# A planner that holds mixer steps back less, and expects later blocks later

## The chip, the cores and the metric

The kernel runs on one core of a Trainium2 chip. The metric is the device time of one execution in microseconds (us). Times inside the profile count from the first instruction of the profiled execution.

## The reference

Two blocks follow each other. The first is a gated delta rule over 768 steps, for 4 batches of 8 heads with 48 dimensions each; the second is a token and channel mixer over the result, laid out as (4, 768, 384).

```python
k_n = k / (norm(k) + 1e-6)
state = 0                                   # (B, H, 48, 48)
for t in range(768):
    y[t] = q[t] @ state
    state += beta[t] * outer(k_n[t], v[t] - k_n[t] @ state)
x = y as (B, 768, 384)
u = x + (x.T @ U @ V).T                     # rank 32
out = u + relu(u @ w_ch1) @ w_ch2           # 384 -> 1536 -> 384
```

The arithmetic is fp32; some inputs are held in 64-bit floats, and the channel weights are converted on the chip.

## The kernel before, in words

**Work.** The sequence of a batch is cut into 12 chunks of 64 steps. Half a batch, six chunks, is a unit; so there are eight units, n = 0 to 7, two for each batch b. For each unit the kernel loads keys, queries and values (`load_keys`, `load`, `turn_all`), forms the products of keys with keys and queries with keys (`grams`, PSUM tile `p_g`, L561), and inverts a triangular matrix for each chunk and head (`blocks`). The inversion goes: key products to DRAM and back in another layout (`scr`, then `gs`, L633 and L644, issued by SP), norms (L652 to L666, `p_n`), a chain of small subtractions on VectorE (L704 and L710), the result to DRAM and back (L719, then `zt` at L782 or `zt` and `zc` at L731 and L734), and then the halves of a block are joined by matmuls. Units 0 to 2 invert in halves of 16 and join them in three thirds (`join`, tiles `p_e`, `p_d`, `p_x`, `p_v`, L842 to L888). Units 3 to 7 invert blocks of 32 and join once, inside `blocks` (`p_x` L746, `p_v` L760); they return before `("compact", n)` is emitted.

**Recurrence.** `recur(b)` walks the 12 chunks of a batch. A chunk is a chain of three groups of TensorE matmuls with an evacuation after each: `p_y` from the state (L909), VectorE's `rhs` (L936), `p_s` (L943), ScalarE's `z` (L952), `p_s` and `p_y` (L957, L965), VectorE's new state (L980). A unit's first chunk needs its joined blocks, `("below", n, third)`.

**Mixer.** When a batch's recurrence is over, `front(b, i)` makes the rank-32 product and transposes (`p_tt` L1007 and L1016, `p_h` L1031, `p_u` L1041) and `wide(b, i)` the two channel products for half a batch: 36 matmuls into `p_f` (L1080), evacuated by ScalarE's ReLU (L1059), and 36 into `p_o` (L1101), added on VectorE and stored (L1064, L1065). The mixer of a batch runs beside the recurrence of the next.

**What sets the order.** The program is written out by a planner, `run()`. Every part is a generator. It yields `need(...)`, events that it must wait for, or `step(...)`, a piece of work with its estimated cost on each engine (`pe`, `dve`, `act`, `sp`, `pool`), PSUM banks that it takes or gives, and `then`, the time after which its result is expected. `emitted(key, after)` records when an event is expected. The planner keeps a clock for each engine and always emits the step that can start first. `best` is that step; if a part with a lower place, hence more urgent, has a step for the same engine that can start soon enough, that one is emitted instead, and the engine is planned to wait for it:

```python
for other in could:
    early = clock["slow"] > 1.0 or other[1][0] < 5
    if early and engine and other[2] == engine and other[1] < i:
        if other[0] < at + 0.4 * waits[i][engine]:
            best = other
            break
```

`clock["slow"]`, a factor on TensorE's costs, is 1.6 until `front(0, 0)` begins and 1.0 from then on. A mixer step has three products at an estimated 1.95 us; only the `p_f` steps of `wide(0, 1)` are one product each (0.65). Parts with a place of 5 or more (the recurrence of batches 1 to 3, at 5.01 to 5.03, and the blocks of units 3 to 7, at 5.6 and more) are not held for once the mixer runs; unit 2's joins (2.9 to 3.1), the keys, loads and products of units 2 and 3 (below 4), the fronts (1.5) and the evacuations (1) are. The planned clock decides only the order in which instructions stand in each engine's queue; on the chip each engine takes its queue in that order and waits on semaphores.

Of the kernel before, what the change touches and what calls it, by code (L numbers as in the profile page):

```python
# [27 lines left out]
def kernel(  # L28
# [78 lines left out]
    clock = dict(now=0.0, at=0.0, pe=0.0, dve=2.5, act=0.8, sp=0.8, pool=3.8, slow=1.6)  # L107
# [6 lines left out]
    def need(*keys):  # L114

        return [k for k in keys if all(x >= 0 for x in k[1:])]

    def step(pe=0, dve=0, act=0, sp=0, pool=0, then=0.0, on=None, take=(), give=(), ins=64):

        return dict(
            pe=pe, dve=dve, act=act, sp=sp, pool=pool, then=then, on=on, take=take, give=give, ins=ins
        )

    def emitted(key, after=0.0):
        done[key] = clock["at"] + after

    parts, waits, ready = {}, {}, {}

    def advance(i, at):
        clock["at"] = at
        try:
            waits[i], ready[i] = next(parts[i]), at
        except StopIteration:
            del waits[i]
# [9 lines left out]
    def fetched(at, s, goes=False):  # L146

        left = LOT - lot["used"]
        if s["ins"] >= left:
            ahead = s["pe"] * clock["slow"] * left / s["ins"]  # L150
            at = max(at, lot["since"] + FETCH - ahead)
            if goes:
                lot.update(since=at + ahead, used=s["ins"] - left)
        elif goes:
            lot["used"] += s["ins"]
        return at

    def run():

        while waits:  # L160
            best, could = None, []
            for i in sorted(waits):
                while isinstance(waits.get(i), list) and all(k in done for k in waits[i]):
                    advance(i, max([ready[i]] + [done[k] for k in waits[i]]))
                if isinstance(waits.get(i, []), list):
                    continue
                s = waits[i]
                if any(len(free[t]) < s["take"].count(t) for t in s["take"]):
                    continue
                engine = next((e for e in ENGINES if s[e]), None)  # L170
                at = max(
                    [ready[i], clock[engine] if engine else 0.0]
                    + [sorted(free[t])[s["take"].count(t) - 1] for t in s["take"]]
                )
                if s["pe"]:
                    at = fetched(at, s)
                could.append((at, i, engine))
                if best is None or at < best[0] - 1e-6:
                    best = at, i, engine
            if best is None:  # L180
                continue

            at, i, engine = best
            for other in could:
                early = clock["slow"] > 1.0 or other[1][0] < 5
                if early and engine and other[2] == engine and other[1] < i:
                    if other[0] < at + 0.4 * waits[i][engine]:
                        best = other
                        break
            at, i, _ = best  # L190
            s = waits[i]
            for t in s["take"]:
                free[t].remove(min(free[t]))
            ends = {"pe": at}
            if s["pe"]:
                fetched(at, s, True)
                ends["pe"] = clock["pe"] = at + s["pe"] * clock["slow"]
            for e in ENGINES[1:]:
                if s[e]:
                    ends[e] = clock[e] = max(clock[e], ends["pe"]) + s[e]  # L200
            clock["now"] = max(ends.values())
            for t in s["give"]:
                free[t].append(clock["now"] + 0.1)
            advance(i, ends.get(s["on"], clock["now"]) + s["then"])
# [11 lines left out]
    for g in range(2):  # L216
        at = slice(L * g, L * g + L)
# [393 lines left out]
    def blocks(n):  # L611
# [5 lines left out]
        pool, tag = (mix, "ut") if n == 1 else (single, None)  # L617
        def room():

            return [pool.tile([NP, BK + 1, BK], FP32, name=x, tag=tag or x) for x in ("gs", "xt")]  # L620
# [19 lines left out]
        if n > 1:  # L640
            yield need(("inverted", n - 1))
            gs, xt = room()
        yield step(sp=0.4, pool=0.9 if n > 1 else 0, on="sp", then=3.2)
        nc.sync.dma_start(out=gs[:, 0:BK], in_=scr)  # L644
        if n > 1:
            nc.gpsimd.memset(xt, 0.0)
# [133 lines left out]
        yield step(sp=1.1 if n == 0 else 2.2 if n < 2 else 3.2, act=1.1 if n == 0 else 0)  # L780
        for i in range(4):
            two[i % 2].dma_start(out=diagonal(zt, i), in_=blk[i])  # L782
        emitted(("compact", n), 3.2)
        for third in range(3):
            begin(join(n, third, pg, zt), 2.3 + 0.1 * (3 * n + third))

# [21 lines left out]
    def join(n, third, pg, zt):  # L808

        SB, TQ = BK // 2, CS // 3

        bank, ps_of = ("mix", ps_mix) if n < 2 else ("one", ps_one)

        def room(shape, name):
            if n < 2:
                return mix.tile(shape, FP32, name=name, tag="h_f", bufs=12)
            return single.tile(shape, FP32, name=name, tag="xz")

        qs = slice(TQ * third, TQ * third + TQ)
        where = [(e // 4, e // 2 % 2, e % 2) for e in range(TQ * third, TQ * third + TQ)]
        zq = zt.rearrange("p c j r t -> p (c j r) t")[:, qs]

        odd = zq.rearrange("p q (a u s) -> p q a u s", a=2, u=2)[:, :, :, 1]
        yield need(("compact", n))
        if n == 0 and third > 0:
            yield need(("below", 0, 0))
        if (n, third) == (0, 0):
            gated[1] = slice(96, 128), zq[96:128, 0, BK : BK + 1]  # L830
            emitted(("gate", 1))
        if n == 1:
            at = 1536 + TQ * L * third
            zn = early[:, at : at + TQ * L].rearrange("p (q t) -> p q t", q=TQ)
        yield step(pe=0.7 if n < 2 else 0.6, dve=0.0, then=0.1, take=(bank,))
        if n != 1:
            zn = single.tile([128, TQ, L], FP32, name="zn", bufs=2)
        p_e = ps_of([128, TQ, 2, SB], "p_e")
        for e, (c, j, r) in enumerate(where):
            for g in range(2):  # L840
                rows = half(g)
                nc.tensor.matmul(  # L842
                    p_e[rows, e], pg[rows, c, j, r], odd[rows, e], start=True, stop=True
                )

        xe = room([128, TQ, 2, SB], "xe")
        yield step(act=0.65, dve=0.75, then=0.1, give=(bank,))
        turned(zn, zq)
        for a in range(2):
            nc.scalar.mul(xe[:, :, a], p_e[:, :, a], mask_e[:, a : a + 1])  # L850
        yield step(pe=0.7 if n < 2 else 0.6, then=0.1, take=(bank,))
        p_d = ps_of([128, TQ, 2, SB], "p_d")
        for e in range(TQ):
            for g in range(2):
                nc.tensor.matmul(  # L855
                    p_d[half(g), e], zn[half(g), e], xe[half(g), e], start=True, stop=True
                )
        yield step(dve=1.2, then=-0.75, give=(bank,))
        nc.vector.tensor_tensor(out=odd, in0=odd, in1=p_d, op=ALU.subtract)
        turned(zn, zq)  # L860
        yield step(pe=0.7 if n < 2 else 0.6, then=0.1, take=(bank,))
        p_x = ps_of([128, TQ, BK], "p_x")
        for e, (c, j, r) in enumerate(where):
            for g in range(2):
                rows = slice(L * g + BK, L * g + L)
                nc.tensor.matmul(  # L866
                    p_x[L * g : L * g + BK, e],
                    pg[rows, c, j, r, 0:BK],
                    zq[rows, e, BK:L],
                    start=True,  # L870
                    stop=True,
                )
        xz = room([128, TQ, BK], "xz")
        yield step(act=0.75, then=0.1, give=(bank,))
        for g in range(2):
            nc.scalar.copy(xz[L * g : L * g + BK], p_x[L * g : L * g + BK])
        yield step(pe=0.7 if n < 2 else 0.6, then=0.1, take=(bank,))
        p_v = ps_of([128, TQ, BK], "p_v")
        for e in range(TQ):
            for g in range(2):  # L880
                rows = slice(L * g, L * g + BK)
                nc.tensor.matmul(  # L882
                    p_v[rows, e], zn[rows, e, 0:BK], xz[rows, e], start=True, stop=True
                )
        yield step(act=0.75, give=(bank,))
        for g in range(2):
            rows = slice(L * g, L * g + BK)
            nc.scalar.mul(zq[rows, :, BK:L], p_v[rows], -1.0)  # L888
        emitted(("below", n, third), 0.2)
# [232 lines left out]
    for n in range(2, 2 * B):  # L1122
        at = 0.01 * n + (3 if n < 4 else 5)
# [42 lines left out]
```

## Time and profile before

| | |
|---|---|
| median of 6 runs | 666.22 us (663.95 to 668.38) |
| the profiled execution | 665.22 us |
| its span, first to last instruction | 663.5 us |
| mean granted TensorE clock | 0.902 |
| TensorE busy (PE) | 620.1 us, 93% |
| VectorE busy (DVE) | 317.6 us, 48% |
| GpSimd busy (POOL) | 228.6 us, 34% |
| ScalarE busy (ACT) | 169.9 us, 26% |
| DMA | 47.81 MB, mean 72 GB/s |

PE is TensorE's matmuls, PEld its weight loads. The page's second part cuts the span into 40 slices of 16.6 us, and PEclk there is the clock that was granted, in tenths of full speed. The chain is the work that ended last, followed back from the last instruction. In the timeline a row is a group of instructions of one line: start, duration, then in brackets how long the engine sat idle before it and what ended that. A row of stretches gives, for each, its length and then for PE, PEld, DVE, ACT and POOL the busy time with the count of instructions, and at the end the granted clock, the DMA share and GB/s. An fp32 product shows as two matmul records.

### The profile page before, as it was taken

To read this page: it belongs to the slowest core of one execution; us is meant where nothing else is said; L and a number is where in the kernel's file an instruction comes from. 1 tells how busy PE (TensorE), PEld (TensorE's weight loads), DVE (VectorE), ACT (ScalarE), POOL (GpSimd) and SP (SyncE) were. 2 spreads that over 40 slices of the span, in tenths; PEclk is the share of its full clock that TensorE was granted. 3 is DMA by queue.
4 is the path that set the end of the run, shared out by engine and by line. 5 is a ranking of instruction groups with operands and counts; after the bars stand their busy time and mean duration, and the time that the engine had idled before them with its cause. 6 is when DMAs were issued, how large, how long until landed. Compare 5 with 4: busy or idle time off the path is not lost.

```text
span 663.5 us, 19841 instructions
## 1 busy us (share of the span) xinstructions
PE 620.1 (93%) x8736; PEld 399.5 (60%) x8736; DVE 317.6 (48%) x761; ACT 169.9 (26%) x430; POOL 228.6 (34%) x380
## 2 busy tenths in 40 slices
PE   4659997798999999989999999999999999999997
PEld 3548896466765565555556555555565555555554
DVE  3478778786278608845852585348611012000000
ACT  3413454133421331134211321232212211110210
POOL 9544068770671573265519151700000000000000
PEclk9765555598599999999999999999999999999999
DMA  8864358732431371184126223320120000000000
GB/s 119 182 156 84 113 138 198 211 81 72 109 83 41 96 134 29 34 152 81 36 62 129 66 38 72 86 62 2 41 47 14 2 13 12 13 0 25 12 12 25
DMA packets 85159, 47.81 MB, mean 72 GB/s; under 512 B 73584, under 2 KB 78240, under 8 KB 85072
## 3 DMA queue, kind: packets, MB, share of 16 engines
q0 software_dynamic: 14528, 26.98, 17.4%
q1 hardware_dynamic: 65808, 18.86, 13.3%
q8 instruction: 69, 1.13, 0.7%
q10 hardware_dynamic: 4736, 0.69, 0.6%
q14 instruction: 18, 0.15, 0.1%
HBM read 35.49 MB, written 11.01 MB: 70 GB/s over the span
## 4 chain that ended last, share of the span: by engine, by line
PE 86%; DMA 5%; DVE 3%; POOL 3%; issue 2%; ACT 1%; SPq 0%; ACTq 0%; POOLq 0%; DVEq 0%
PE p_f L1080 30%; PE p_o L1101 30%; PE p_y L909 4%; PE p_g L561 3%; PE p_s L943 3%; PE p_s L957 2%; PE p_e L842 2%; PE p_d L855 2%; PE p_y L965 2%; DMA kn<-in_k_dram 1%; PE p_u L1041 1%; PE p_v L882 1%; PE p_h L1031 1%; POOL qn L494 1%; PE p_x L866 1%
## 5 line engine op out<-in xcount | busy, mean ns | idle before, releaser
L1080 PE MATMUL p_f<-ut,w_sb 128*128 128x384 f32 x576 | 204.3, 501 | 0.0
L1101 PE MATMUL p_o<-w_sb,h_f 128*128 128x384 f32 x576 | 203.1, 497 | 0.0
L1080 PEld LDWEIGHTS p_f<-ut,w_sb 128*128 128x128 f32 x576 | 105.4, 191 | 64.7 <-issue 1.2
L1101 PEld LDWEIGHTS p_o<-w_sb,h_f 128*128 128x128 f32 x576 | 104.3, 190 | 65.3 <-issue 2.9
L1059 ACT ACTIVATE h_f<-p_f 128x384 f32<-128x384 f32 x96 | 47.1, 490 | 177.9 <-PE p_f L1080 177.7
L1064 DVE TENSOR_TENSOR x<-x,p_o 128x384 f32<-128x384 f32 x24 | 13.2, 554 | 148.3 <-PE p_o L1101 148.3
L494 POOL DMA_DIRECT2D qn<-in_k_dram x96 | 58.4, 617 | 46.3 <-DVE qt L503 18.3
L710 DVE TENSOR_TENSOR xt<-xt,prod 96x112 f32<-96x112 f32 (+21 forms) x200 | 63.7, 318 | 6.9
L494 POOL DMA_DIRECT2D qn<-in_q_dram x96 | 59.0, 622 | 22.4 <-DVE kt L503 18.5
L433 POOL DMA_DIRECT2D vn<-in_v_dram x64 | 41.9, 666 | 71.8 <-DVE rhs L936 32.7
L704 DVE TENSOR_TENSOR prod<-gs,xt 96x112 f32<-96x112 f32 (+21 forms) x200 | 63.1, 316 | 5.2
L987 ACT COPY x<-p_y 64x192 f32<-64x192 f32 x96 | 30.0, 313 | 55.8 <-PE p_y L965 53.9
L952 ACT COPY z<-p_s 128x192 f32<-128x192 f32 x48 | 15.3, 318 | 94.9 <-PE p_s L943 94.6
L936 DVE TENSOR_TENSOR rhs<-vn,p_y 128x192 f32<-128x192 f32 x44 | 15.4, 350 | 42.8 <-PE p_y L909 42.5
L433 POOL DMA_DIRECT2D kn<-in_k_dram x48 | 31.8, 673 | 2.0 <-DMA qn<-in_q_dram 1.3
L980 DVE TENSOR_TENSOR s<-s,p_s 128x192 f32<-128x192 f32 x40 | 14.0, 351 | 35.7 <-PE p_s L957 29.7
L957 PEld LDWEIGHTS p_s<-z,kn 64*64 64x64 f32 x704 | 17.4, 153 | 22.6 <-issue 16.3
L943 PEld LDWEIGHTS p_s<-rhs,zt 64*64 64x64 f32 x704 | 16.9, 153 | 23.2 <-issue 16.1
L909 PEld LDWEIGHTS p_y<-s,kt 48*64 48x64 f32 x704 | 17.5, 153 | 20.6 <-issue 8.7
L957 PE MATMUL p_s<-z,kn 64*64 64x48 f32 x704 | 23.0, 248 | 4.5 <-ACT z L952 4.5
L943 PE MATMUL p_s<-rhs,zt 64*64 64x48 f32 x704 | 22.6, 248 | 4.5 <-DVE rhs L936 4.5
L909 PE MATMUL p_y<-s,kt 48*64 48x48 f32 x704 | 23.4, 248 | 2.3 <-ACT x L987 1.8
(126 smaller groups left out, 638.4 us busy)
## 6 DMA issues: line engine op xcount, KB each, us to landing
wide<-in_moe_w_ch_dram POOLq DMA_DIRECT2D x7, 768.0 KB, 5.5
vn<-in_v_dram POOLq DMA_DIRECT2D x64, 72.0 KB, 3.2
out_dram<-x SPq DMA_DIRECT2D x24, 192.0 KB
kn<-in_k_dram POOLq DMA_DIRECT2D x48, 72.0 KB, 3.6
gs<-scr SPq DMA_DIRECT2D x8, 384.0 KB
scr<-xt SPq DMA_DIRECT2D x8, 384.0 KB
scr<-pg SPq DMA_DIRECT2D x30, 96.0 KB
zt<-scr SPq DMA_DIRECT2D x30, 96.0 KB
```

The source lines that it names most:

```text
L433: engines[queue].dma_start(out=t[half(g ^ (s % 2) if crossed else g), :, s], in_=src[b, 4 * g + s, hf * UC * L : (hf + 1) * UC * L, :].rea ...
L494: nc.gpsimd.dma_start(out=places[rows, x, j, :, 0 : ds.stop - ds.start], in_=src[b, h, hf * UC * L : (hf + 1) * UC * L, ds].rearrange("(m ...
L561: nc.tensor.matmul(p_g[par][to, c, j], kq[0][rows, x, j, c0 + c], kq[i][rows, x, j, c0 + c], start=True, stop=True,)
L704: nc.vector.tensor_tensor(out=prod, in0=gb[:, :, j : j + 1, j + 1 :].to_broadcast([NP, split, m, w]), in1=xb[:, :, 0:m, j : j + 1].to_broa ...
L710: nc.vector.tensor_tensor(out=xb[:, :, 0:m, j + 1 :], in0=xb[:, :, 0:m, j + 1 :], in1=prod, op=ALU.subtract,)
L909: nc.tensor.matmul(p[half(x ^ par), par, D * (2 * i + j) : D * (2 * i + j) + D], kq[i][half(par, D), x, j, cu], s_old[half(par, D), x, j], ...
L943: nc.tensor.matmul(p_s[half(x), par, D * (2 + j) : D * (2 + j) + D], zt[half(x ^ par), cu, j, par], rhs[half(x ^ par), 2 * j + par], start ...
L957: nc.tensor.matmul(p_s[half(par), x, D * j : D * j + D], kn[half(x), cu, 2 * j + par], z[half(x), 2 * j + par], start=True, stop=True,)
L987: nc.scalar.copy(tokens_of(b, c, g), pair_of(p_y, 1)[half(g)])
L1059: nc.scalar.activation(hs[f], p_f, ACTF.Relu)
L1080: nc.tensor.matmul(p_f, w1_sb[:, t, f * 128 : (f + 1) * 128], ut[:, t], start=(t == 0), stop=(t == KT - 1),)
L1101: nc.tensor.matmul(p_os[c], hs[e][:, c * 128 : c * 128 + 128], w2_sb[:, e], start=(e == 0), stop=(e == FT - 1),)
```

## The change

It has four parts. The planner's wait for a more urgent step stays 0.4 of the waiting step's cost until the mixer runs, and is at most 0.1 us from then on. For units 2 to 7 the load of `gs` is expected after 4.9 us instead of 3.2. For unit 2 `("compact", n)` is expected after 4.7 us instead of 3.2. And in the joins of unit 2 the result of each matmul group is expected after 0.4 us instead of 0.1, in all four groups. No instruction is added or removed, and no tile or queue is changed: only the order in each queue.

```diff
@@ run()
             for other in could:
                 early = clock["slow"] > 1.0 or other[1][0] < 5
                 if early and engine and other[2] == engine and other[1] < i:
-                    if other[0] < at + 0.4 * waits[i][engine]:
+                    wait = 0.4 * waits[i][engine]
+                    if other[0] < at + (wait if clock["slow"] > 1.0 else min(wait, 0.1)):
                         best = other
                         break
@@ blocks(n)
-        yield step(sp=0.4, pool=0.9 if n > 1 else 0, on="sp", then=3.2)
+        yield step(sp=0.4, pool=0.9 if n > 1 else 0, on="sp", then=3.2 if n < 2 else 4.9)
         nc.sync.dma_start(out=gs[:, 0:BK], in_=scr)
...
-        emitted(("compact", n), 3.2)
+        emitted(("compact", n), 3.2 if n < 2 else 4.7)
@@ join(n, third, pg, zt): the steps of p_e, p_d, p_x and p_v
-        yield step(pe=0.7 if n < 2 else 0.6, dve=0.0, then=0.1, take=(bank,))
+        yield step(pe=0.7 if n < 2 else 0.6, dve=0.0, then=0.4 if n > 1 else 0.1, take=(bank,))
...
-        yield step(pe=0.7 if n < 2 else 0.6, then=0.1, take=(bank,))
+        yield step(pe=0.7 if n < 2 else 0.6, then=0.4 if n > 1 else 0.1, take=(bank,))
```

The line numbers in the text are those of the kernel before; from the second line of the edit in `run()` on, a line of the changed kernel stands one further down.

More of the change, by code (lines that the diff above doesn't have):

```diff
@@ L860, in join @@
         turned(zn, zq)
-        yield step(pe=0.7 if n < 2 else 0.6, then=0.1, take=(bank,))
+        yield step(pe=0.7 if n < 2 else 0.6, then=0.4 if n > 1 else 0.1, take=(bank,))
         p_x = ps_of([128, TQ, BK], "p_x")
@@ L876, in join @@
             nc.scalar.copy(xz[L * g : L * g + BK], p_x[L * g : L * g + BK])
-        yield step(pe=0.7 if n < 2 else 0.6, then=0.1, take=(bank,))
+        yield step(pe=0.7 if n < 2 else 0.6, then=0.4 if n > 1 else 0.1, take=(bank,))
         p_v = ps_of([128, TQ, BK], "p_v")
```

## The prediction

> **What bounds the kernel now.** I read the page first: busy shares, slices, chain.
>
> ```profile
> PE 620.1 (93%) x8736; PEld 399.5 (60%) x8736; DVE 317.6 (48%) x761; ACT 169.9 (26%) x430; POOL 228.6 (34%) x380
> PE   4659997798999999989999999999999999999997
> PEclk9765555598599999999999999999999999999999
> PE 86%; DMA 5%; DVE 3%; POOL 3%; issue 2%; ACT 1%; SPq 0%; ACTq 0%; POOLq 0%; DVEq 0%
> ```
>
> TensorE holds 86% of the chain, and from slice 12 (counted from 0; 200 us) it is all but full. Its work is the same before and after (576 p_f and p_o products, 288 each), so a new order can gain or lose in three ways only: time in which PE idles, time at the half clock (the 5 in PEclk), and breaks in the mixer's stream. The change acts once the mixer runs (128 us on), so the second 5 of PEclk, slice 10, is the first place to look. The timeline of PE there (start, us, engine, line, operation, count of records; an fp32 product is two):
>
> ```profile
> 156.09 2.06 PE L842 MATMUL p_e<-zt,pg 64*64 64x32 f32 x64
> 157.98 1.10 PE L855 MATMUL p_d<-xe,zn 64*64 64x32 f32 x32
> 159.87 1.92 PE L855 MATMUL p_d<-xe,zn 64*64 64x32 f32 x32 [0.78 <-ACT xe L850]
> 161.71 1.92 PE L866 MATMUL p_x<-zt,pg 32*32 32x32 f32 x64
> ...
> 165.62 1.06 PE L882 MATMUL p_v<-xz,zn 32*32 32x32 f32 x32 [0.89 <-ACT xz L876]
> ...
> 175.87 4.21 PE L1080 MATMUL p_f<-ut,w_sb 128*128 128x384 f32 x6
> 180.00 0.58 PE L943 MATMUL p_s<-vn,zt 64*64 64x48 f32 x16
> 180.52 2.20 PE L1080 MATMUL p_f<-ut,w_sb 128*128 128x384 f32 x6
> ```
>
> Unit 2's joins run as one block from 156.05, with no mixer product between them. The second p_d takes 1.92 for what took 1.10 before, and three p_f products take 4.13 (175.94 to 180.07) where 2.13 is normal: the block runs at half clock. Windows of one clock step (3.41 us) show where it falls and where it does not:
>
> ```profile
> 156.53:159.94 3.41, 2.63 (x90) 2.51 (x88) 0.78 (x2) 1.41 (x5) 0.00 (x0) 0.99 0.03 5
> 159.94:163.36 3.42, 3.42 (x94) 3.36 (x96) 1.85 (x4) 0.47 (x2) 0.00 (x0) 0.50 0.00 0
> 286.22:289.63 3.41, 2.33 (x71) 1.46 (x64) 2.13 (x2) 1.00 (x4) 2.30 (x4) 1.00 0.57 158
> ```
>
> The first (PE busy 2.63, all small tiles) costs the clock; it comes back at 180.42. The third is busy for less (2.33) and keeps it; some 1.1 of that is wide p_tt. So the mix counts, not only busy time. That third window is the end of the recurrence of batch 1, where the mixer of batch 0 has run out:
>
> ```profile
> 283.94 0.45 PE L943 MATMUL p_s<-rhs,zt 64*64 64x48 f32 x16
> 284.88 0.45 PE L957 MATMUL p_s<-z,kn 64*64 64x48 f32 x16 [0.49 <-ACT z L952]
> 285.93 0.45 PE L909 MATMUL p_y<-s,kt 48*64 48x48 f32 x16 [0.37 <-DVE s L980]
> 287.18 0.45 PE L943 MATMUL p_s<-rhs,zt 64*64 64x48 f32 x16 [0.57 <-DVE rhs L936]
> 288.14 0.45 PE L965 MATMUL p_y<-z,qk 64*64 64x48 f32 x16 [0.51 <-ACT z L952]
> 288.52 1.66 PE L1007 MATMUL p_tt<-x,u_sb 128*32 128x384 f32 x12
> ```
>
> Each uncovered link of the recurrence leaves PE idle for 0.4 to 0.6.
>
> **What the Trainium skill says.** "TensorE: Matmul & The Clock Gate", section "What's actually happening", has the clock halved after an idle window of about 3.4 us and restored after a busy one, the windows free-running. The trace agrees: the half-clock stretch from 159.94 to 180.42 is 20.48, six windows. It also shows that a window of small matmuls (2.63 of 3.41) counts as idle. The same page, table of specifications, has ScalarE and VectorE as strict FIFO; here ACT and DVE wait only for the head of their order, as the idle entries show. So I follow each queue below.
>
> **The change, part by part.** The orders of the two built programs differ only from the first front on.
>
> 1. *Holding back.* A mixer step (three products, model cost 1.95) was held for a more urgent one due within 0.4 x 1.95 = 0.78; now within 0.1. The old order of unit 2's joins was p_e 32, p_d 32, p_x 32, p_v 32, p_e 16, key products (p_g) 16, p_d 16, p_x 16, p_g 16, p_v 16, p_g 16, then p_f. The new one puts three p_f after the first p_e, after p_d with p_g, after p_x with p_g and a half of p_v, and then three p_o between nearly all the rest. p_e starts after the same 27 p_f products (about 156), after the landing that ended a wait at 154.66, so the later due times alone move nothing there.
>    Price: elapsed 156.05 to 180.07 is 24.0, for 112 join products, 48 p_g and 3 p_f. At full clock, without the waits: p_e 2.0 + 1.0 and p_d 1.93 + 0.96 (rows at 156.09 and 157.98); p_x and p_v 1.9 together, from unit 4's p_x, the same 32*32 tiles, 96 records from 296.93 to 297.87 at full clock (p_v likewise); p_g 48 at 0.59 per 16 = 1.77 (row at 290.11); p_f 2.13. Sum 11.7. **Gain 12.3** if the clock holds; not below 2, since the three waits (0.78, 0.89, 0.52) get 2 us of mixer as cover. I take 12.3: the worst new window, p_d 32 with p_g 32, has 1.2 of dense 64-wide p_g and at least 0.2 of p_f in it, more than the window that kept the clock has beside its p_tt.
>    Behind the moved steps, with the new order laid out from 156 by these durations: on DVE the keys' transpose of unit 3 (1.77) now precedes the two transposes of joins; p_d has 2.1 of p_f as cover. The third join's subtraction waits for p_d to about 174 with the last weight slice's five passes (4.0) queued behind it; they end near 179, p_o of f = 9 to 11 comes near 187, and norm (L654), behind them, near 182, p_n near 184. ACT's norm (L652) for unit 3 stands ahead of a join's copy: key products end near 167, the gs load takes 10 from there as before (176.6 to 186.4), so it is there at 177 to 178, when ACT reaches it. All held, by 1 to 6 us.
> 2. *Breaks.* The mixer's stream is cut into 131 runs instead of 125. Three products after a small group take 2.13, in a run 23.22 / 12 = 1.94: 6 x 0.19 = **loss 1.1**.
> 3. *Front of batch 0.* Two query groups stand ahead of p_h, and p_f between the transposes covers the 0.29 wait at 140.13: **gain 0.3**, between -1 (p_h waits for the qk products on DVE) and 0.5.
> 4. *End of the recurrence of batch 1.* The mixer of batch 0 is used up earlier: the new order has two more links uncovered, so idle 0.49 + 0.37 + 0.1 more than the 1.94 shown. Then unit 4's blocks: DVE transposes zc at 298.49, released by the DMA, and p_v (L760) runs at 301.50. Inversion end to that transpose is 285.47 to 298.49, 13.0, none of it PE's. All of unit 4's chain moves up with its PE inputs by about 10, but p_x and p_v now stand directly behind p_u and p_h without p_f between: wait about 2.5. And now 6 to 7 us pass with recurrence tiles and p_g alone and 2.9 idle, so a free-running window can fall wholly inside and cost the clock. From p_tt to p_u it then takes 124.01 to 136.13 = 12.1 as in the first front at half clock, against 288.52 to 295.78 = 7.3: 4.8 more, part of which covers the wait of 2.5. **Loss 1 to 8; I take 5.**
> 5. *Later due times (gs 4.9, compact 4.7, joins 0.4) and queues.* No order of units 3 to 7 has the joins any more (L724 returns before). gs moves p_n one recurrence step later, beside mixer products. On SP the beta load of unit 3 (3.06 of issue) goes behind gs: SP sits idle from 153 to 176 anyway, and beta lands 3.6 after, near 181, for use near 182. On POOL the xt memsets (1.0) shift by two to eight query loads of 0.62; POOL is idle for 15 at a time there. Zero, with 1 us either way: their cover is the 9 or so us between the DMA's end and p_x in units 5 to 7.
> 6. *Fronts of batches 2 and 3.* p_o between the transposes covers waits of 0.24 at 433.97, 554.22 and 560.58: **gain 0.5** (0 to 0.7). From 567 on both orders are the same 96 us of mixer.
>
> Sum: 12.3 - 1.1 + 0.3 - 5.0 + 0.5 = 7.0. The profiled execution took 665.22 (span 663.5 and 1.7 around it), so 658.2; the median of the runs, 666.22, is 1.0 above it: **659.2**.
>
> **Rivals.**
> - *The clock holds at item 4 too*: loss 1 to 2 there, total gain 10 to 11, about 656. For it: 286.22 kept its clock. Chance 0.27, against 0.40 for the forecast.
> - *The clock falls in the joins anyway.* Then one to three groups of p_f and p_o run at 4.13 rather than 2.13, item 1 brings about 4, and the sum is 4 - 1.1 + 0.3 - 5 + 0.5, a loss of 1.3: 667.5. For it: 40 to 128 us stay at half clock with PE 97% busy at 80 to 100. Against: after p_f at 175.94 it recovered at once. Chance 0.17.
> - *Slower: unit 4's chain does not move up.* If its gs or zc transfers stay put (their SP queue is nearly packed, 226.87 to 246.2), p_v cannot come before 299, while 6 fewer mixer products are done by then; the 12 of item 1 are lost in that wait, and breaks and half clock remain: 4 more, 670. It decides once the chain moves up by less than 5. Against: inversion 3 begins after p_n, which moves with PE. Chance 0.11.
> - Anything else 0.05; that the order does not change is excluded by the built programs.
>
> **The numbers.** A measurement of this kernel can tell about 0.5%, 3.3 us: faster means below 662.9, slower above 669.5. Faster: 0.37 of the 0.40, all of 0.27, 0.03 of the third and a part of the rest, 0.68. Slower 0.12, same 0.20. The range leaves out the slow rival and little else: 654.5 to 667.5; the forecast's own is 657 to 662.5.
>
> **What would show it.** Right: no 5 in PEclk after slice 7; no p_f or p_o group of 4 us between 156 and 185; the first p_tt of batch 1 near 278; idle before p_v of unit 4. Wrong at step 1: half clock between 160 and 180 again. Wrong at step 4: no idle and no half clock between 270 and 295 (faster than forecast), or p_tt near 278 but the first p_s of batch 2 still near 306.

## The result, and the profile after

| | before | after |
|---|---|---|
| median of all runs beside each other | 665.16 us (661.52 to 674.59, 72 runs) | 661.65 us (655.07 to 666.69, 35 runs) |
| ratio after/before, 95% interval | | 0.9926 [0.9909, 0.9943] |
| profiled execution / its span | 665.22 / 663.5 us | 666.69 / 664.9 us |
| mean granted TensorE clock | 0.902 | 0.897 |

The change makes the kernel faster by 0.74%, some 4.9 us (0.0074 x 665.16). The ratios, and the medians of the clock further down, leave out the runs that were more than 1.5% above the fastest of their kernel, four of the 35 here; the medians in the table keep them and differ by 3.5 us. The profiled execution of the changed kernel is the longest of its 35 runs, so its trace shows where time can be lost and not what a usual run loses. The page of the changed kernel, the same lines as before:

```profile
PE 621.1 (93%) x8736; PEld 398.5 (60%) x8736; DVE 317.8 (48%) x761; ACT 169.8 (26%) x430; POOL 228.5 (34%) x380
PE   4659897699999999889999999999999999999997
PEclk9755555679999999958999999999999999999999
PE 86%; DMA 7%; DVE 4%; ACT 1%; SPq 1%; issue 1%; POOL 0%; ACTq 0%; DVEq 0%
```

The 5 of slice 10 has gone from PEclk. In its place there is a low clock in slices 17 and 18 (283 to 316 us), where before had 9s. In this profile the clock in unit 2's joins was won for all but one window, and a new loss came at the end of batch 1's recurrence. The timeline of PE in the changed kernel, first the joins (start, us, engine, line, operation, records):

```profile
156.68 2.06 PE L843 MATMUL p_e<-zt,pg 64*64 64x32 f32 x64
158.67 2.20 PE L1081 MATMUL p_f<-ut,w_sb 128*128 128x384 f32 x6
160.80 1.12 PE L856 MATMUL p_d<-xe,zn 64*64 64x32 f32 x32
162.71 1.06 PE L856 MATMUL p_d<-xe,zn 64*64 64x32 f32 x29 [0.79 <-ACT xe L851]
...
165.32 3.20 PE L1081 MATMUL p_f<-ut,w_sb 128*128 128x384 f32 x6
168.45 1.20 PE L867 MATMUL p_x<-zt,pg 32*32 32x32 f32 x64
...
184.06 4.14 PE L1102 MATMUL p_o<-w_sb,h_f 128*128 128x384 f32 x12
```

Mixer products now stand between the join groups. One p_f group takes 3.20 where 2.20 is normal: the clock was at half from 164.0 to 167.4, one window, against six (159.9 to 180.4) before. Then the end of the recurrence of batch 1:

```profile
275.27 0.45 PE L958 MATMUL p_s<-z,kn 64*64 64x48 f32 x16
275.54 0.41 PE L966 MATMUL p_y<-z,qk 64*64 64x48 f32 x16
276.27 0.45 PE L910 MATMUL p_y<-s,kt 48*64 48x48 f32 x16 [0.31 <-DVE s L981]
...
276.77 0.66 PE L562 MATMUL p_g<-qt,kt 48*64 48x64 f32 x32
279.01 0.45 PE L944 MATMUL p_s<-rhs,zt 64*64 64x48 f32 x16 [1.59 <-DVE prod L705]
279.94 0.68 PE L958 MATMUL p_s<-z,kn 64*64 64x48 f32 x16 [0.48 <-ACT z L953]
...
284.67 2.77 PE L1008 MATMUL p_tt<-x,u_sb 128*32 128x384 f32 x12
...
302.33 2.88 PE L1081 MATMUL p_f<-ut,w_sb 128*128 128x384 f32 x6
```

More links stand without a mixer product than before, and the wait of 1.59 is new: a product `p_g` of unit 4's queries stands ahead of `p_s`. VectorE finishes evacuating it (`qk`, 278.12 to 278.86) just before `p_s` starts, with small steps of unit 4's inversion ahead of that. From 279.94 on the small groups take 0.68 where they took 0.45; the clock comes back at 303.9. The stretches show it: first the window of one clock step that ended at 280.05, then what followed (length, PE busy and count, PEld, DVE, ACT, POOL, granted clock, DMA share, GB/s):

```profile
276.64:280.05 3.41, 1.34 (x75) 1.11 (x69) 3.17 (x13) 0.34 (x2) 0.00 (x0) 0.99 0.18 62
160.59:164.00 3.41, 2.62 (x89) 2.31 (x91) 1.26 (x3) 1.00 (x3) 2.62 (x5) 0.99 0.37 64
280.00:304.00 24.00, 21.55 (x425) 13.93 (x426) 7.31 (x14) 7.50 (x18) 20.60 (x33) 0.50 0.77 148
```

PE was busy for 1.34 of 3.41 us ahead of the long loss, and for 2.62 ahead of the one-window loss in the joins. During the long one it was busy for 21.55 of 24 us and still stayed at half clock.

Cut at the same marks of TensorE's order, the two profiles differ so (us):

| stretch | before | after |
|---|---|---|
| start to p_tt of batch 0 | 124.0 | 123.8 |
| to p_e of unit 2 | 32.1 | 32.9 |
| to p_tt of batch 1 | 132.4 | 128.0 |
| to p_tt of batch 2 | 130.4 (132 mixer products) | 133.4 (126) |
| to p_tt of batch 3 | 125.2 | 124.5 |
| to the end | 119.4 (168) | 122.3 (174) |

### The profile page after: what moved, and what is told of

It reads as the page before. It is cut to its first block, busy times and chain, and to the rows that moved or that the text cites. A ratio compares the mean times of both kernels' runs of the same rounds, so it can differ in the third digit from the quotient of the medians.

```text
span 664.9 us, 19849 instructions
## 1 busy us (share of the span) xinstructions
PE 621.1 (93%) x8736; PEld 398.5 (60%) x8736; DVE 317.8 (48%) x761; ACT 169.8 (26%) x430; POOL 228.5 (34%) x380
## 3 DMA queue, kind: packets, MB, share of 16 engines
q8 instruction: 69, 1.13, 0.7%
## 4 chain that ended last, share of the span: by engine, by line
PE 86%; DMA 7%; DVE 4%; ACT 1%; SPq 1%; issue 1%; POOL 0%; ACTq 0%; DVEq 0%
PE p_f L1081 30%; PE p_o L1102 30%; PE p_y L910 4%; PE p_g L562 3%; PE p_s L944 3%; PE p_s L958 2%; PE p_e L843 2%; PE p_y L966 2%; PE p_u L1042 2%; PE p_d L856 1%; DMA scr<-pg 1%; DMA zt<-scr 1%; DMA gs<-scr 1%; PE p_h L1032 1%; DMA kn<-in_k_dram 1%; DMA scr<-xt 1%
## 5 line engine op out<-in xcount | busy, mean ns | idle before, releaser
L1081 PE MATMUL p_f<-ut,w_sb 128*128 128x384 f32 x576 | 207.3, 505 | 0.0
L495 POOL DMA_DIRECT2D qn<-in_q_dram x96 | 58.9, 621 | 10.2 <-DVE kt L504 7.1
L958 PEld LDWEIGHTS p_s<-z,kn 64*64 64x64 f32 x704 | 17.7, 155 | 19.6 <-issue 15.2
```

The costliest lines, as they stand in the source:

```text
L495: nc.gpsimd.dma_start(out=places[rows, x, j, :, 0 : ds.stop - ds.start], in_=src[b, h, hf * UC * L : (hf + 1) * UC * L, ds].rearrange("(m ...
L958: nc.tensor.matmul(p_s[half(par), x, D * j : D * j + D], kn[half(x), cu, 2 * j + par], z[half(x), 2 * j + par], start=True, stop=True,)
L1081: nc.tensor.matmul(p_f, w1_sb[:, t, f * 128 : (f + 1) * 128], ut[:, t], start=(t == 0), stop=(t == KT - 1),)
```

## The experiments

Two theories were tested. **The first**, that of the prediction: the shorter holding back puts mixer products between the join groups, which is the gain, and it uses up the mixer before batch 1's recurrence ends, which is the loss; the due times do nothing. **The rival**: the due times bring the gain. Each experiment ran on the same chip as the kernel before. A mixer product in an unbroken run of them is 0.645 us (two records of 128x384 at 0.3225).

**hold**: only the holding back.

```diff
-                    if other[0] < at + 0.4 * waits[i][engine]:
+                    wait = 0.4 * waits[i][engine]
+                    if other[0] < at + (wait if clock["slow"] > 1.0 else min(wait, 0.1)):
```

> Only the planner's wait is capped at 0.1; the due times are those of before. Theory (the gain is the clock in unit 2's joins, part of it lost again at the end of batch 1's recurrence): its joins have the mixer between them as in the changed kernel, and its last five links of that recurrence are uncovered too, so it takes what the changed kernel takes, 658 to 663. Rival (the later due times bring the gain): no gain, 664 to 666.

Measured: 664.07 us, ratio 0.9955 [0.9928, 0.9981]. The median lies above the 658 to 663 of the theory and within the 664 to 666 of the rival. The interval still leaves out 1, so there is a gain, but a smaller one than forecast. The order is as expected. In the profile p_f groups stand between the joins, one of them partly at half clock, and the last links are bare:

```profile
160.00 2.20 PE L1081 MATMUL p_f<-ut,w_sb 128*128 128x384 f32 x6
166.54 3.32 PE L1081 MATMUL p_f<-ut,w_sb 128*128 128x384 f32 x6
...
280.82 0.45 PE L944 MATMUL p_s<-rhs,zt 64*64 64x48 f32 x16 [1.15 <-DVE qk L578]
286.50 2.77 PE L1008 MATMUL p_tt<-x,u_sb 128*32 128x384 f32 x12
```

The clock was at half from 281.5 to 291.7, so the loss at the end of the recurrence is there in this profile too.

**due**: only the three due times.

```diff
-        yield step(sp=0.4, pool=0.9 if n > 1 else 0, on="sp", then=3.2)
+        yield step(sp=0.4, pool=0.9 if n > 1 else 0, on="sp", then=3.2 if n < 2 else 4.9)
...
-        emitted(("compact", n), 3.2)
+        emitted(("compact", n), 3.2 if n < 2 else 4.7)
...
-        yield step(pe=0.7 if n < 2 else 0.6, then=0.1, take=(bank,))
+        yield step(pe=0.7 if n < 2 else 0.6, then=0.4 if n > 1 else 0.1, take=(bank,))
```

> Only the later due times; the planner's wait is 0.4 of a step as before. Its joins of unit 2 stand nearly in one block again (p_e 32, p_g, p_d 32, p_g, p_x 32, p_v 32), but every link at the end of batch 1's recurrence has three mixer products beside it. Theory: half clock in the joins as before, no gain there; 3 to 5 gained at the end of batch 1's recurrence; 660 to 663. Rival (due times do nothing by themselves): 664 to 666. Rival (they bring the whole gain): as the changed kernel or faster, with the clock held between 160 and 180.

Measured: 659.59 us, ratio 0.9901 [0.9863, 0.9939]. The due times alone bring as much as the whole change (the intervals overlap), and the holding back alone brings less. The clock fell in its joins for one window (163.8 to 167.2) and not for six as before. The timeline of PE in this kernel, at the end of batch 1's recurrence:

```profile
270.07 2.20 PE L1101 MATMUL p_o<-w_sb,h_f 128*128 128x384 f32 x6
272.20 0.45 PE L943 MATMUL p_s<-rhs,zt 64*64 64x48 f32 x16
272.58 2.20 PE L1101 MATMUL p_o<-w_sb,h_f 128*128 128x384 f32 x6
274.71 0.45 PE L965 MATMUL p_y<-z,qk 64*64 64x48 f32 x16
275.09 2.20 PE L1101 MATMUL p_o<-w_sb,h_f 128*128 128x384 f32 x6
277.22 1.48 PE L1007 MATMUL p_tt<-x,u_sb 128*32 128x384 f32 x12
```

Every one of the last links has a mixer group beside it, and no idle entry stands in brackets. In the order of this kernel the recurrence of batch 1 begins after 27 products of batch 0's mixer, in the changed kernel after 36: nine more are left to cover its end.

**filljoin**: the kernel before with an unused matmul of 128x384 after each group in unit 2's three joins, 12 in all (7.7 us at 0.645), to see what the lost clock there costs.

```diff
+    def fill(cols=384):
+        p_fill = ps_mix([128, cols], "p_fill")
+        nc.tensor.matmul(p_fill, ident, w1_sb[:, 0, 0:cols], start=True, stop=True)
...
+        if n == 2:
+            fill()
```

> The kernel before, with one wide matmul (128x384, its result is not used) after each of the 12 groups of unit 2's joins; the order is otherwise the same. It adds 12 x 0.65 = 7.7 of work and hides at most the 2.2 of waits there. Theory (the clock counts): full clock through the joins gives back some 8 to 10, so 663 to 667 and no half clock between 160 and 180. Rival (what the mixer products bring in the changed kernel is cover for waits): 670 to 672.

Measured: 668.85 us, ratio 1.0042 [1.002, 1.0065], between the two forecasts. The clock stayed at full from 128.1 to the end in its profile. An added matmul takes more there than 0.645, though: from its start to the next one's it is 0.84, between two small groups.

```profile
155.17 0.91 PE L810 MATMUL p_fill<-w_sb,ident 128*128 128x384 f32 x2
156.01 1.12 PE L846 MATMUL p_e<-zt,pg 64*64 64x32 f32 x32
```

The 12 take 10.2 together and cost 2.8 (0.0042 x 665.65), so about 7 came back. Up to 2.2 of that are waits of the joins that the added work filled (0.78, 0.89 and 0.52 in the profile before). The clock lost in before's joins is thus worth an estimated 5 to 7 us of a usual run, less than the 10 that half of its 20.5 us would be.

**fillend**: the changed kernel with six unused matmuls of 128x256 at the uncovered links of batch 1's recurrence (`fill()` as above, with 256 columns). They were reckoned at 0.43 us each; in its profile each takes 0.63 from its start to the next one's, 3.8 in all.

```diff
+                if b == 1 and c > 9:
+                    fill()
...
+            if b == 1 and c > 9:
+                fill()
...
+            if b == 1 and c in (9, 10):
+                fill()
```

> The changed kernel, with six matmuls of 128x256 (0.43 each, result not used) beside the uncovered links at the end of batch 1's recurrence; all else in the same order. Theory (the loss there is half clock, 24 us of it in the profile of the changed kernel): the clock holds, 4 to 7 faster than the changed kernel, 655 to 658. Rival (the loss is waits and unit 4's chain of blocks, which do not depend on the clock): the same as the changed kernel or up to 2 slower, 661 to 664.

Measured: 657.02 us, ratio 0.9862 [0.9835, 0.9889]. With more work the kernel is faster than the changed kernel by 0.64% (0.9926 less 0.9862), 4.3 us. The timeline of PE shows why; p_fill is the added matmul:

```profile
273.98 0.70 PE L908 MATMUL p_fill<-w_sb,ident 128*128 128x256 f32 x2
274.61 0.69 PE L562 MATMUL p_g<-qt,kt 48*64 48x64 f32 x32
276.27 0.45 PE L950 MATMUL p_s<-rhs,zt 64*64 64x48 f32 x16 [0.97 <-DVE prod L705]
...
281.15 1.66 PE L1018 MATMUL p_tt<-x,u_sb 128*32 128x384 f32 x12
...
292.70 2.10 PE L1091 MATMUL p_f<-ut,w_sb 128*128 128x384 f32 x6
```

The clock is full here throughout: p_tt takes 1.66 (2.77 in the changed kernel) and the first p_f 2.10 (2.88). From p_tt to that p_f it is 11.6 us instead of 17.7. The 0.97 in front of p_s is left.

**fillend_qlate**: the same, with unit 4's third query product held until the recurrence is over, so that it can't stand in front of p_s.

```diff
+            if n == 4 and c0 == 4:
+                yield need(("rec", 3))
```

> The changed kernel with the six extra matmuls at the end of batch 1's recurrence, and with unit 4's third query product moved behind that recurrence. In the changed kernel it stood between p_y and p_s, took the PSUM pair that p_s needs, and p_s waited 1.59 for its evacuation. Theory: 1 to 2 faster than with the extra matmuls alone, 655 to 656. Rival (unit 4's chain of blocks sets the start of batch 2's recurrence anyway): no difference, 657.

Measured: 658.15 us, ratio 0.9895 [0.9856, 0.9933], not separable from fillend. In its profile p_s starts at 275.74 with no idle entry, so that product was the cause of the wait. But the planner also moved other steps (129 products instead of 126 between the p_tt of batches 1 and 2), so what the 0.97 costs in time stays open.

**gs_only**: only the due time of units 2 to 7's `gs`.

```diff
-        yield step(sp=0.4, pool=0.9 if n > 1 else 0, on="sp", then=3.2)
+        yield step(sp=0.4, pool=0.9 if n > 1 else 0, on="sp", then=3.2 if n < 2 else 4.9)
```

> Only the later gs time (4.9). Unit 2's joins stand in one block as before, 23 mixer products stand between unit 4's key products and unit 3's p_x, and the last five links of batch 1's recurrence have no mixer product beside them. Theory: no gain, and 0 to 4 lost at the end of that recurrence, 665 to 669. Rival (it is this part that the due times' gain comes from): 658 to 662.

Measured: 667.64 us, ratio 1.0037 [1.0018, 1.0057], slower. Its order leaves the joins' block as it was and more of batch 1's last links bare (seven idle entries there, 3.25 us, where before had four with 1.94); its profile, which is one of its longest runs, has the half clock in both places, 20.5 and 23.9 us.

**cj_only**: only the two due times of unit 2, the compact blocks' (4.7) and the join groups' (0.4).

```diff
-        emitted(("compact", n), 3.2)
+        emitted(("compact", n), 3.2 if n < 2 else 4.7)
...
-        yield step(pe=0.7 if n < 2 else 0.6, then=0.1, take=(bank,))
+        yield step(pe=0.7 if n < 2 else 0.6, then=0.4 if n > 1 else 0.1, take=(bank,))
```

> Only the two due times of unit 2 (compact 4.7, joins 0.4); gs and the planner's wait as before. Theory (what the due times bring is the cover at the end of batch 1's recurrence, and it comes from unit 2's joins, since batch 1's recurrence starts with fewer mixer products used up): as with all due times, 658 to 662. Rival (the gs time of the later units brings it): no gain, 664 to 667.

Measured: 656.84 us, ratio 0.9881 [0.9836, 0.9926]: at least as much as the whole change, the intervals overlapping.

**compact_only** and **join_only**: one of those two each.

> Only the due time of unit 2's compact blocks (3.2 to 4.7) is changed. Both due times of unit 2 together gave 0.9881 [0.9836, 0.9926]. Theory A (the gain of the pair is a covered end of batch 1's recurrence and mixer products put beside the joins, and the compact blocks' due time alone is enough for both, since its order has one product at each of the last links and the key products stand between the join groups): 0.988 to 0.992, the profile's stretch from p_e of unit 2 to batch 1's p_tt near 124 us, the clock lost for one window at most in the joins and none near 280. Theory B (the joins' own due times carry it): 0.997 to 1.003. Theory C (only the two together give it): both this and the joins' due time alone within 0.995 to 1.0.

> Only the due time of what a join's groups release (0.1 to 0.4, unit 2) is changed. In its order products of the mixer and key products stand between the join groups, but the last links of batch 1's recurrence stand uncovered, as in the changed kernel. Theory A (the compact blocks' due time carries the gain, by the cover at the end of the recurrence): 0.995 to 1.003, with the clock lost from about 280 us for some windows. Theory B (the joins' own due times carry it, the uncovered links costing little on average): 0.986 to 0.991.

Measured: compact_only 663.18 us, 0.996 [0.9938, 0.9983]; join_only 660.11 us, 0.9906 [0.987, 0.9942]. The theory that the compact blocks' due time carries the gain by its covered end fell. The joins' own due time carries most, though the two intervals just touch. The timelines of PE tell the two apart; first compact_only:

```profile
162.51 1.87 PE L842 MATMUL p_e<-zt,pg 64*64 64x32 f32 x32
164.31 1.06 PE L882 MATMUL p_v<-xz,zn 32*32 32x32 f32 x32
166.44 1.80 PE L855 MATMUL p_d<-xe,zn 64*64 64x32 f32 x29 [1.06 <-ACT xe L850]
...
169.97 4.21 PE L1080 MATMUL p_f<-ut,w_sb 128*128 128x384 f32 x6
```

No mixer product stands between these groups, and the p_f that follows takes 4.21: half clock from 161.1 to 174.8, four windows. Then join_only:

```profile
154.27 2.20 PE L1080 MATMUL p_f<-ut,w_sb 128*128 128x384 f32 x6
156.41 1.12 PE L855 MATMUL p_d<-xe,zn 64*64 64x32 f32 x32
158.31 1.06 PE L855 MATMUL p_d<-xe,zn 64*64 64x32 f32 x29 [0.79 <-ACT xe L850]
...
160.32 2.20 PE L1080 MATMUL p_f<-ut,w_sb 128*128 128x384 f32 x6
162.46 1.20 PE L866 MATMUL p_x<-zt,pg 32*32 32x32 f32 x64
163.59 0.69 PE L561 MATMUL p_g<-kt 48*64 48x64 f32 x32
164.21 0.69 PE L882 MATMUL p_v<-xz,zn 32*32 32x32 f32 x32
164.84 2.20 PE L1080 MATMUL p_f<-ut,w_sb 128*128 128x384 f32 x6
```

A p_f group stands after every one to three kinds of small matmuls, and none takes more than 2.20. With the same products in each stretch as before, p_e of unit 2 to p_tt of batch 1 takes 125.0 us (152.29 to 277.34) instead of 132.4. Its last links are uncovered, and they cost one window of clock in its profile (276.3 to 279.7).

**hold_cj**: the changed kernel with the gathers' due time set back, so the holding back and unit 2's two due times together.

```diff
-        yield step(sp=0.4, pool=0.9 if n > 1 else 0, on="sp", then=3.2 if n < 2 else 4.9)
+        yield step(sp=0.4, pool=0.9 if n > 1 else 0, on="sp", then=3.2)
```

> The changed kernel with the due time of unit 3's gathers set back to 3.2 (left are the cap on the holding back and both due times of unit 2). Its TensorE order is nearly that of the changed kernel, with the end of batch 1's recurrence uncovered. Theory A (the cap spends the mixer's products early and so takes part of the gain of the two due times): 0.991 to 0.995, as the changed kernel's 0.9926. Theory B (it was the gathers' due time, slower alone at 1.0037, that took it): 0.986 to 0.990, as the two due times alone.

Measured: 661.28 us, ratio 0.9921 [0.9889, 0.9953], the changed kernel's own figure. This points to the holding back, and not the gathers' due time, as what takes from the gain: 0.9881 without it, 0.9921 with it. It is not shown, since the two intervals overlap.

**due_fill** and **cj_fill**: the three due times, and unit 2's two, each with three unused matmuls of 128x256 where a join group waits for ScalarE.

```diff
+        if n == 2 and third == 0:
+            fill()
...
+        if n == 2 and third == 1:
+            fill()
...
+        if n == 2 and third == 0:
+            fill()
```

> The kernel with the later due times alone, with three matmuls of 128x256 (0.43 each, result not used) at the three waits of PE in unit 2's joins (0.79, 0.38, 0.89 in its profile). Theory (the clock falls in the joins in most runs and costs 2 to 4): 656 to 659, 1 to 3 faster than without them. Rival (the joins no longer matter): 659 to 661.

> The two due times of unit 2 alone, and three more matmuls of 128x256 (0.43 us each, results not used) in unit 2's join groups that wait for ScalarE (1.3 us of work added). Theory A (these waits trip the clock once, for 3.4 us, which costs some 1.7 us, and the added work lies mostly in idle time): 0.984 to 0.988, 653 to 657 us; no half-clock stretch after the first one. Theory B (nothing is left to lose in the joins once key products stand between their groups): 0.988 to 0.991, the added work being paid in full.

Measured: due_fill 655.81 us, 0.9857 [0.9818, 0.9895]; cj_fill 657.62 us, 0.9878 [0.9848, 0.9909]. In cj_fill's profile the clock stayed at full from 129.6 on. Neither differs from its version without the added matmuls (0.9901 and 0.9881) by more than the intervals, 2 to 3 us wide on each side, so what the one window costs that due's and cj_only's profiles lose stays open. The lowest ratios are those of due_fill, fillend, cj_fill and cj_only, 0.9857 to 0.9881, not separable from each other. The intervals of the first two lie below the changed kernel's; those of the other two reach into it, or up to it. cj_only needs no added work.

**What the profiles have in common.** Half-clock time, in us, in the profiles of the kernels that have the same TensorE work (what falls into the last 2 us is left out):

| kernel | first stretches, up to 142 at most | near unit 2's joins | end of batch 1's recurrence | sum | span | ratio of the runs |
|---|---|---|---|---|---|---|
| before | 109.2 | 20.5 | 0 | 129.7 | 663.5 | 1 |
| after | 102.4 | 6.8 (front) + 3.4 | 23.9 | 136.5 | 664.9 | 0.9926 |
| hold | 122.9 | 3.4 | 10.2 | 136.5 | 662.0 | 0.9955 |
| due | 99.0 | 3.4 | 0 | 102.4 | 653.1 | 0.9901 |
| gs_only | 119.5 | 20.5 | 23.9 | 163.8 | 674.9 | 1.0037 |
| cj_only | 102.4 | 3.4 | 0 | 105.8 | 653.8 | 0.9881 |
| compact_only | 102.4 | 13.7 | 0 | 116.1 | 657.9 | 0.996 |
| join_only | 102.4 | 0 | 3.4 | 105.8 | 653.3 | 0.9906 |
| hold_cj | 102.4 | 6.8 (front) + 3.4 | 10.2 | 122.9 | 661.7 | 0.9921 |

A straight line through before's point with 0.37 us of span for each us at half clock gives the other spans within 1.4 us, hold alone being off by 4.0 (gs_only: 34.1 x 0.37 = 12.6, measured 11.4; due: -27.3 x 0.37 = -10.1, measured -10.4). The Trainium skill, "TensorE: Matmul & The Clock Gate", section "Terms", prices time at half clock at one half of itself; 0.37 is below that, which fits a TensorE that also waits in these stretches. The first column is lost almost wholly in work that stands in the same order in all of these kernels, and still it differs by 24 us (99.0 to 122.9). That is as large as the effects sought, so one profile of each kernel can rank the mechanisms but not size them; the ratios do that.

**What the other runs show.** The mean granted clock of every run is on record, and 2 x (1 - clock) x span is the run's half-clock time (changed kernel, profiled: 2 x 0.1027 x 664.9 = 136.6, against 136.5 in the table). Medians over the runs, less the medians of the kernel before beside them, in us:

| kernel | half-clock time | span |
|---|---|---|
| hold | -5.5 | -1.9 |
| due | -13.7 | -6.1 |
| gs_only | +8.9 | +2.0 |
| cj_only | -18.3 | -9.4 |
| compact_only | -6.7 | -2.8 |
| join_only | -14.2 | -5.8 |
| hold_cj | -10.2 | -5.9 |
| filljoin (work added) | -18.9 | +3.1 |
| fillend (work added) | -28.2 | -9.4 |

A few runs whose record reads 0.98 or more without their being faster are left out. 0.45 us of span for each us at half clock gives the seven without added work within 2.1. So the link of time and clock is not one of single profiles only. Within the runs of one kernel the slope is 0.24 (286 runs taken together), so part of what parts the kernels is something else that goes with the clock, waits that the same order covers for one; how much is not settled. The median of the changed kernel is 114.1 us and that of fillend 98.5. A usual run of the changed kernel thus loses some 16 us of clock that the six matmuls keep, and not the 34.1 of its profile (6.8, 3.4 and 23.9).

**Do the parts add?** The three due times do: -0.94% (joins), -0.40% (compact blocks) and +0.37% (gathers) sum to -0.97%, measured together -0.99%, each of these known to 0.2 to 0.4%. The holding back doesn't: -0.45% and -0.99% would give -1.44%, measured -0.74%. In both orders of the joins, hold's and join_only's, p_f groups stand after p_e and after p_d with p_g, so the second part finds little left to gain there. That explains why the gains don't add, and not why hold brings less than join_only: the last links of both are bare. Their orders also differ in the fronts, where hold has query products ahead of p_h, and in one more bare link; which of these takes from hold's gain was not tried.

## Why the prediction was right or wrong

**The total was right**, 659.2 with 654.5 to 667.5, against 661.65, and faster as forecast: 4.9 us by the ratio against 7.0 of the sum. The reason for it was half right, and that the total came out near is in part luck: the joins were priced too high by 4 us or more, and the due times, worth 6.6 us by themselves (0.0099 x 665.65), at nothing. Of the four signs that were to show it right one came, no p_f group of 4 us between 156 and 185. A 5 stands in slice 17, the first p_tt of batch 1 came at 284.67 and not near 278, and no idle entry stands before p_v of unit 4.

- **Item 1, joins, +12.3: mis-sized.** In the changed kernel 156.68 to 184.12 is 27.4; less five of its six groups of three mixer products at 2.13 (10.7; the sixth has its like in before's stretch), and less 1.0 for recurrence groups, the same joins took 15.7, against 24.0: 8.3 gained in these two profiles. Three terms failed. p_x and p_v were priced by unit 4's 96-record groups; the row at 168.45 has 64 in 1.13 (to the next start at 169.58), and with four rows of 32 at 0.62 the 192 records took 3.6 and not 1.9. One window lost the clock (1.7), and one wait of 0.79 stayed. In usual runs it may be less again: in filljoin only about 7 came back in all. (The 112 join products of the text should be 192, as its own list adds up; the sum does not use the figure.)
- **Item 5, later due times, zero: wrong, and the main error.** The sentence that the later due times "alone move nothing there" was argued from when p_e starts. They do not move p_e; they move what stands between the groups after it, since a group that is expected 0.3 later lets a mixer step go first. join_only is -0.94% on its own. I had compared only the two whole orders and gave the difference to the edit that reads most like it. Nor did the orders differ only from the first front on: with the later gathers ScalarE takes the recurrence's z ahead of unit 2's norm at 116.54, where before had norm first.
- **Item 4, end of batch 1's recurrence, -5: right in kind, and in size for the usual run.** The clock did fall there, in the profile for 23.9 us. That profile lost about 9.9: 6.9 from p_tt to p_tt (133.4, plus 3.9 for six products fewer, less 130.4) and 3.0 in the links ahead. fillend puts the usual loss at 4.3 or more. The wait of unit 4's chain (2.5) did not come; its p_x stands at 297.18 with no wait entry. The chain moved up by 5.2 and not by 10, and with the clock at half the first p_s of batch 2 came only 1.0 earlier (305.80 instead of 306.80). The new wait was another: 1.59 for VectorE behind p_g, which no step had.
- **Item 3, +0.3: wrong sign in this profile.** From p_tt to p_e it took 32.9 instead of 32.1; a p_f group at 136.18 took 4.11, at half clock from 133.3 to 140.1. But that stretch took 30 to 36 us in the other runs, so the size is not settled. **Item 6, +0.5:** 0.7 from p_tt of batch 2 to that of batch 3 (125.2 to 124.5). **Item 2, -1.1:** not tried by itself.
- **The rivals.** That the clock holds at the end of the recurrence happened in no profile of a kernel with the holding back, unless work was added there (fillend). That it falls in the joins anyway happened for one window. Unit 4's chain did move up, by little more than the 5 that this rival named: its last small subtraction ended at 280.29 instead of 285.47.

What stays open: where a usual run of the changed kernel loses its clock, since the other runs have only the mean; what the holding back costs besides; and what the 1.59 wait costs by itself.

## What to carry to other kernels

When a planner's constants are changed together, build each constant alone before giving the gain to one: here the edits overlapped, and unit 2's two due times without the other two edits were at least as good as all four. Where small matmuls stand in a block, ask what wide matmul follows each of them, and whether work that is put there is missing as cover later. Size a clock effect by the ratio of many runs, since much the same work lost between 99 and 123 us of clock before the change acts.

## What the runs showed of the hardware

- **Busy time alone does not decide whether a window keeps the clock.** Of stretches of one window, those of before (2.63 busy, shown with the prediction) and the changed kernel (2.62, shown above) lost it; in join_only a window that lies in the joins too kept it (the rows are cut within 0.22 us of the clock's own steps):

```profile
272.63:276.04 3.41, 1.99 (x96) 1.65 (x96) 1.66 (x6) 0.95 (x3) 0.12 (x1) 1.00 0.41 119
...
156.69:160.10 3.41, 2.62 (x120) 2.51 (x120) 1.72 (x4) 1.92 (x5) 2.85 (x5) 1.00 0.30 62
```

  The second row has the same 2.62 and kept the clock. The first row, the uncovered links, lost it from 276.3 on. One measure parts the windows better: the rows of the array that each matmul record uses times the columns that it streams (128 x 384 for p_f, 64 x 32 for p_e), summed over a window. Cut at the clock's own steps, from 125 to 560 us in the fourteen profiles, the 16 windows that lost the clock have 98 to 233 thousand (before 178, the changed kernel's joins 211), and of the 1690 that kept it all but four (205 to 212) have more than 233 (join_only 291). These sums are estimates from the durations of the traces, and no run varies the measure by itself. The Trainium skill, "TensorE: Matmul & The Clock Gate", section "What's actually happening", speaks of an idle window; here windows with PE busy for three quarters counted as such.
- **A lost clock can stay lost under load.** PE was busy for 21.55 of 24.0 us in the changed kernel and the clock came back only at 303.9, within the first p_f group. In the profile before, six windows in a row had PE busy throughout, at half clock:

```profile
77.94:98.42 20.48, 20.48 (x579) 19.28 (x576) 15.55 (x29) 9.63 (x26) 10.68 (x18) 0.50 0.42 115
```

  So that the clock comes back after a busy window, as the prediction has it, does not hold here if busy means that PE has work. In fillend six matmuls of 128x256, 0.63 us each, at the bare links were enough to keep it.
- **The half-clock stretches after 128 us are 3.4, 6.8, 10.2, 13.7, 20.5 and 23.9 us**, all multiples of 3.41.
